# The denominator of linear attention, batches 3 to 7: from TensorE matmuls to GpSimd products and VectorE sums

## The chip, the cores and the metric

The kernel runs on one core of one Trainium2 chip. Its engines work side by side and meet at semaphores: PE (TensorE, matrix products into PSUM), DVE (VectorE), ACT (ScalarE), POOL (GpSimd) and SP (SyncE, which here only issues DMAs). The metric is the device time of one execution in microseconds; lower is better. The kernel before takes 287.69 us, the median of three runs (287.32 to 287.95).

## The reference

Linear attention over 8 batches, 8 heads, 576 tokens and 64 dimensions per head, and behind it a feed-forward layer over all 4608 tokens:

```python
def phi(x):
    return np.where(x > 0, x, np.exp(x) - 1.0) + 1.0
q_p, k_p = phi(q), phi(k)
kv  = np.einsum('bhsd,bhse->bhde', k_p, v)
z   = np.sum(k_p, axis=2)
num = np.einsum('bhsd,bhde->bhse', q_p, kv)
den = np.einsum('bhsd,bhd->bhs', q_p, z)[..., None] + 1e-06
x   = (num / den) reshaped to [4608 tokens, 512]
h   = x @ w_in              # 512 -> 2048
out = (h - np.tanh(h)) @ w_out   # 2048 -> 512
```

The denominator is one number for each token and head. It may divide `num` at the end, or, since `num` is linear in phi(q), it may divide phi(q) ahead of the product with kv.

## The kernel before

**The feed-forward part** goes over nine chunks (`c`) of 512 tokens. In the first half of a chunk, 16 slots (`s1[0]` to `s1[15]`, one for each 128 rows of h) hold four matmuls each (`l1mm`, line 366). After every second slot `l1act2` (lines 372 and 373) lets ACT take the tanh of a pair of PSUM banks and DVE subtract it into `gT`. The pairs go round in banks 0 to 5 of PSUM, so the matmuls of a pair need the subtraction of three pairs earlier. In the second half, 16 slots (`s2[0]` to `s2[15]`) hold four matmuls each (`l2mm`, line 387); after every fourth, `evac` copies a result out of PSUM on ACT (line 396) and SP sends it to DRAM (line 403).

**The attention part** of later batches is sewn into those slots. The lists `s1` and `s2` hold functions that issue their instructions behind the matmuls of a slot; each engine and each DMA queue works in that written order, so the order of the slots is the order of the work. With `n1 = c + 1` and `n2 = c + 2`, chunk c does this:

- At `s1[0]` GpSimd loads k, q and v of batch n2 (lines 87 and 90, a DMA with a cast to bf16). Ahead of the loads stands `gate` (line 383): GpSimd copies one element of the transposed q of batch n1, so the loads wait until that transpose has landed.
- At `s1[8]` (`s1[10]` in chunk 1) `a_den` makes the denominators of batch n1: 16 matmuls of a 128x32 stationary tile (line 287), then an addition of 1e-6 and a reciprocal on DVE (lines 292 and 296). `a_spread` sends the reciprocals to DRAM (`ds`, line 316) and reads them back, spread over the partitions, as `rdb` (line 319), by DMAs that SP issues.
- At `s2[2]` to `s2[8]` ACT and DVE make phi(k) and phi(q) of batch n2 (lines 129 to 131) and DVE copies v (`a_vp`, line 190). At `s2[8]` SP issues the DMA that transposes phi(q) of n2 into `qT` (`a_qT_dma`, line 148).
- At `s2[9]` (`s2[12]` in chunk 1) `a_num` has PE compute num of n1 from `qT` (lines 228 and 236), then kv and z of n2 (`kv_cols_mm`, line 177). DVE multiplies num by `rdb` on its way from PSUM to `xT` (lines 333 and 338), which drains PSUM banks 0 to 3 that the next chunk's first slots write. Last, `kz_copy` brings kv and z of n2 to SBUF; z is laid out as 32 columns by a product with a mask (line 199), kv is copied (line 200).

The next chunk's `l1mm` reads `xT` of batch n1. The buffers `kraw` and `qraw` are single, so a load of k or q can't begin before phi of the batch ahead has read them. Batches 0, 1 and 2 have paths of their own around chunks 0 and 1, which the change leaves as they are.

Of the kernel before, what the change touches and what calls it, by code (L numbers as in the profile page):

```python
# [11 lines left out]
F32 = mybir.dt.float32  # L12
# [6 lines left out]
def kernel(  # L19
# [9 lines left out]
    nc = tc.nc  # L29
# [5 lines left out]
    NF = DF // 128  # L35
    NC = N // 512
    J = S // 64


    const = ctx.enter_context(tc.tile_pool(name="const", bufs=1))  # L40
# [52 lines left out]
    def load_k(b):  # L93
        k_t[b] = kpool.tile([128, 2, 2, J, D], BF16, name="kraw")
        load(b, k_t[b], k, b == 0)

    def load_q(b):
        q_t[b] = kpool.tile([128, 2, 2, J, D], BF16, name="qraw")
        load(b, q_t[b], q, b == 0)

    def load_v(b):
        load(b, v_b[b % 2][:, 0:2], v, b == 0)
# [9 lines left out]


    kp_t, qp_t, qT_t, kz_t, rdb_t, rden_t = {}, {}, {}, {}, {}, {}

    def phi_pieces(b, src, store, name, i, parts=0):

# [22 lines left out]
    def a_qphi(b, i):  # L140
        phi(b, q_t, qp_t, "qp", i)
# [4 lines left out]
    def a_qT_dma(b):  # L146
        new_qT(b)
        nc.sync.dma_start_transpose(
            out=qT_t[b].rearrange("p i j g t -> p (i j) (g t)"),
            in_=qp_t[b].rearrange("p i j h d -> p (i j h d)"))  # L150
# [41 lines left out]
    def kv_cols_mm(b, b0, o):  # L192
        kz_t[b] = kz_c[b % 2]
        kv_mm(b, lambda rs, h, i, j: vp[rs, i, j, h, :],
              lambda cs, hg, i: ps_all[cs, b0 + hg, o + 66 * i:o + 66 * i + 66])

    def kz_copy(b, b0, o):
        ps = ps_all[:, b0:b0 + 2, o:o + 132].rearrange("p g (i e) -> p g i e", i=2)
        nc.vector.tensor_mul(kz_t[b][:, :, :, 64:96], ps[:, :, :, 64:65].to_broadcast([128, 2, 2, 32]), mask)
        nc.vector.tensor_copy(kz_t[b][:, :, :, 0:64], ps[:, :, :, 0:64])  # L200


    def b0_z(i):
# [74 lines left out]
    def a_den(b, bank, parts=range(4)):  # L278

        kz, qT = kz_t[b], qT_t[b]  # L280
        ps = ps_all[:, bank, 0:J * 16]
        for t in range(4) if b == 0 else ():
            nc.tensor.matmul(ps[32 * t:32 * t + 32], eps[:, 0:32], one[:, 0:J * 16], start=True, stop=False)
        for n, p in enumerate((0, 2, 1, 3)):
            if n in parts:
                for t in range(4):
                    nc.tensor.matmul(ps[32 * t:32 * t + 32], kz[:, p // 2, p % 2, 64:96],  # L287
                                     qT[:, p % 2, :, p // 2, 16 * t:16 * t + 16],
                                     start=(n == 0 and b > 0), stop=(n == NP - 1))
        if b > 0:  # L290
            den = rpool.tile([128, J * 16], F32, name="den")
            nc.vector.tensor_scalar(den, ps, 1e-6, None, ALU.add)
        else:
            den = ps
        rden = rpool.tile([128, J * 16], F32, name="rden")
        nc.vector.reciprocal(rden, den)  # L296
        rden_t[b] = rden
# [14 lines left out]
    def a_spread(b):  # L312

        ds = dram.tile([H, 4, J * 16], F32, name="ds")
        for t in range(4):
            nc.sync.dma_start(out=ds[:, t, :], in_=rden_t[b][32 * t:32 * t + H, :])
        rdb = rpool.tile([128, NP, 4, J, 16], F32, name="rdb")
        for hh in range(2):
            nc.sync.dma_start(
                out=rdb[64 * hh:64 * hh + 64].rearrange("p a t j c -> p (a t j c)"),  # L320
                in_=ds[4 * hh:4 * hh + 4].rearrange("h t c -> (h t c)").partition_broadcast(64))
        rdb_t[b] = rdb

    def a_num(b, nxt):

        rdb = rdb_t[b]
        for i in range(2):
            num_mm(b, i, lambda h: 2 * h + i)
        rest = rest_mm(b, 6, 0)
        if nxt:  # L330
            kv_cols_mm(nxt, 6, 128)
        for n in range(NP):
            nc.vector.tensor_mul(  # L333
                xT[:, n, S * b:S * b + 512].rearrange("p (j t c) -> p j t c", j=8, t=4),
                ps_all[:, n, :].rearrange("p (j t c) -> p j t c", j=8, t=4),
                rdb[:, n, :, 0:8, :].rearrange("p t j c -> p j t c"))
        for h in range(2):
            nc.vector.tensor_mul(
                xT[:, 2 * h:2 * h + 2, S * b + 512:S * b + 576].rearrange("p a (t c) -> p a t c", t=4),
                rest[h].rearrange("p a (t c) -> p a t c", t=4), rdb[:, 2 * h:2 * h + 2, :, 8, :])  # L340
        if nxt:
            kz_copy(nxt, 6, 128)

    def new_ns(b):

# [34 lines left out]
    def gate(qT):  # L380

        g0 = rpool.tile([1, 1], BF16, name="g0")
        nc.gpsimd.tensor_copy(g0, qT[0:1, 1, J - 1, 1, 63:64])  # L383
# [6 lines left out]
    def evac(c, i, o, f0=0, f1=None):  # L390
        f1 = DM if f1 is None else f1
        osb = opool.tile([128, DM], F32, name="osb")
        if f0:
            nc.vector.tensor_copy(osb[:, f0:f1], o[:, f0:f1])  # L394
        else:
            nc.scalar.copy(osb[:, f0:f1], o[:, f0:f1])  # L396

        last = c == NC - 1 and i == 3
        for half in range(2):
            b, j = divmod(2 * (4 * c + i) + half, J)  # L400
            cuts = [f0, 256, f1] if c == 3 and i < 3 else [f0, f1]
            for a0, a1 in zip(cuts, cuts[1:]):
                (nc.scalar if last and half else nc.sync).dma_start(
                    out=out[b * S:(b + 1) * S, a0:a1].rearrange("(p j) m -> p j m", j=J)[:, j, :],
                    in_=osb[64 * half:64 * half + 64, a0:a1])
# [103 lines left out]
    for c in range(NC):  # L509
# [4 lines left out]
        if c == 0:  # L514
            sub = {}

            def spread1(h):
                sub["bp"] = a_spread_pe(1, 4, (2 * h, 2 * h + 1))
                for p in (2 * h, 2 * h + 1):
                    a_scale(1, p, sub["ns"], sub["bp"], 144 * (p % 2))  # L520

            def num1():
                ns = sub["ns"] = new_ns(1)
                for h, ps in enumerate(rest_mm(1, 6, 128)):
                    nc.scalar.copy(ns[:, 2 * h:2 * h + 2, 8, :], ps)
                for i in range(2):
                    b0 = 4 + 2 * i
                    num_mm(1, i, lambda h: b0 + h)
                    nc.scalar.copy(ns[:, i::2, 0:8, :].rearrange("p a j t -> p a (j t)"), ps_all[:, b0:b0 + 2, :])

            s1[11].append(lambda: a_kphi(1, 0))
            s1[13].append(lambda: a_kphi(1, 1))
            s2[3].append(lambda: a_qphi(1, 0))
            s2[4].append(lambda: (a_qphi(1, 1), load_q(2), load_k(2), load_v(2)))
            s2[0].append(prepare)
            s2[7].append(lambda: (a_qT_pe(1, 0, Banks([4, 5])), a_kv(1, 6), a_qT_pe(1, 1, Banks([4, 5]))))
            s2[8].append(lambda: (scale_rest(0, 6, rdb_t[0]), a_den(1, 4), num1(), a_split(1)))
            s2[10].append(lambda: spread1(0))

            qs, ks = [], []  # L540

            def exp2(pieces, src, store, name, i):
                pieces.append(phi_pieces(2, src, store, name, i))
                pieces[i][0]()

            def rest2(f):
                f[1]()
                f[2]()

            s2[11].append(lambda: exp2(qs, q_t, qp_t, "qp", 0))  # L550
            s2[12].append(lambda: (spread1(1), exp2(qs, q_t, qp_t, "qp", 1), rest2(qs[0])))
            s2[13].append(lambda: (exp2(ks, k_t, kp_t, "kp", 0), rest2(qs[1]), a_qT_dma(2)))
            s2[14].append(lambda: rest2(ks[0]))
        elif n1 < B:
            if c == 1:
                s1[8].append(lambda: (kv_cols_mm(2, 6, 0), kz_copy(2, 6, 0)))
            s1[10 if c == 1 else 8].append(lambda: (a_den(n1, 6), a_spread(n1)))
            s2[12 if c == 1 else 9].append(lambda: a_num(n1, n2 if n2 < B else 0))
        if c == 1:
            s1[1].append(lambda: a_kphi(2, 1))  # L560
            s1[3].append(lambda: (a_vp(2, 0), a_vp(2, 1)))
        if c >= 1 and n2 < B:

            s1[0].append(lambda: (gate(qT_t[n1]), load_k(n2), load_q(n2), load_v(n2)))
            d = 2
            s2[d].append(lambda: a_kphi(n2, 0))
            s2[d + 2].append(lambda: a_kphi(n2, 1))
            s2[d + 4].append(lambda: a_qphi(n2, 0))
            s2[d + 6].append(lambda: (a_qphi(n2, 1), a_qT_dma(n2)))
            for i in range(2):  # L570
                s2[d + 1 + 2 * i].append(lambda i=i: a_vp(n2, i))
        if c == 0:
# [93 lines left out]
```

## Time and profile before

| | |
|---|---|
| median of the runs | 287.69 us (287.32 to 287.95) |
| the profiled execution's own time | 287.78 us |
| its span, first to last instruction | 286.0 us |
| mean granted TensorE clock | 0.998 |
| PE busy | 276.8 us (97%) |
| DVE busy | 171.3 us (60%) |
| ACT busy | 139.6 us (49%) |
| POOL busy | 30.0 us (10%) |
| GpSimd's DMA queue (loads), share of 16 DMA engines | 39.5% |
| SP's DMA queue (the rest), share of 16 DMA engines | 30.8% |

The profile is one execution of the program, with times in microseconds from the span's start. A group line gives the line of the code, the engine and operation, written and read tile, shape and count, then busy time and the mean duration in ns of one instruction, and behind the second bar the idle time just ahead of them and who ended it. The chain of waits is followed backwards from the last instruction. A timeline line gives start, duration, and in square brackets an idle time with what ended it. In a timeline's line for several instructions the duration is that from the start of the first to the end of the last. Neighbouring instructions of one engine can overlap by a little.

### The profile page before, as it was taken

What the parts mean: (1) busy time and instruction counts of PE and PEld (TensorE: products, weight loads), DVE (VectorE), ACT (ScalarE), POOL (GpSimd) and SP (SyncE); (2) the same over time, 40 slices, a digit from 0 to 9 for tenths busy, and PEclk for the clock granted to TensorE, in tenths of its full rate; (3) what the DMA queues carried; (4) which work ended last, traced back from release to release, by engine and by line L of the source; (5) the groups of instructions that cost most, each with busy time, mean ns of one, the idle gap of its engine ahead of it and who ended that gap; (6) DMA issues with size and microseconds to landing.
All of it is one profiled execution on the core that took longest, in us unless ns stands there. A gap on an engine that the chain in (4) does not pass through costs nothing.

```text
span 286.0 us, 5195 instructions
## 1 busy us (share of the span) xinstructions
PE 276.8 (97%) x2127; PEld 130.8 (46%) x2155; DVE 171.3 (60%) x271; ACT 139.6 (49%) x167; POOL 30.0 (10%) x50
## 2 busy tenths in 40 slices
PE   8889999999999999999999999999999999999995
PEld 3544464444444444445444544444444444444443
DVE  3749977997558782877277727874680467006600
ACT  4848557857335643564355625661551155126411
POOL 8642030120030003000300030000000000000000
PEclk9999999999999999999999999999999999999999
DMA  6999999997979668955996679656126210230032
GB/s 98 197 206 213 208 207 208 233 179 147 235 148 207 162 102 151 222 127 132 147 208 148 145 142 216 148 126 138 39 75 138 68 37 0 52 82 16 0 76 73
DMA packets 39496, 38.99 MB, mean 136 GB/s; under 512 B 16368, under 2 KB 34608, under 8 KB 38704
## 3 DMA queue, kind: packets, MB, share of 16 engines
q0 software_dynamic: 17488, 18.35, 39.5%
q1 hardware_dynamic: 21824, 20.17, 30.8%
q8 instruction: 17, 0.28, 0.4%
q10 hardware_dynamic: 160, 0.13, 0.1%
q14 instruction: 7, 0.06, 0.1%
HBM read 43.91 MB, written 9.55 MB: 187 GB/s over the span
## 4 chain that ended last, share of the span: by engine, by line
PE 93%; DMA 2%; issue 1%; POOL 1%; DVE 1%; DVEq 0%; POOLq 0%
PE ps_all L366 43%; PE ps_all L387 42%; DMA v<-in_v_dram 2%; PE ps_all L177 2%; PE ps_all L228 1%; PE ps_all L622 1%; PE ps_all L287 1%; PE ps_all L251 1%; POOL kraw L87 1%; DVE xT L255 0%; POOL qraw L87 0%; PE ps_all L159 0%; DVE rden L296 0%; PE ps_all L236 0%; PE ps_all L354 0%
## 5 line engine op out<-in xcount | busy, mean ns | idle before, releaser
L366 PE MATMUL ps_all<-xT,w_in_sb 128*128 128x512 bf16 x559 | 125.4, 379 | 1.2 <-issue 0.5
L387 PE MATMUL ps_all<-w_out_sb,gT 128*128 128x512 bf16 x547 | 122.2, 379 | 1.3 <-issue 1.0
L373 DVE TENSOR_TENSOR gT<-ps_all,th 128x1024 bf16<-128x1024 f32 x64 | 77.8, 1217 | 66.7 <-ACT th L372 66.7
L372 ACT ACTIVATE th<-ps_all 128x1024 f32<-128x1024 f32 x64 | 65.5, 1023 | 50.1 <-PE ps_all L366 50.1
L366 PEld LDWEIGHTS <-w_in_sb 128*128 128x128 bf16 x574 | 55.4, 98 | 67.1 <-issue 0.6
L387 PEld LDWEIGHTS <-gT 128*128 128x128 bf16 x560 | 54.1, 98 | 64.4 <-issue 0.2
L396 ACT COPY osb<-ps_all 128x512 f32<-128x512 f32 (+1 forms) x36 | 20.8, 582 | 74.0 <-PE ps_all L387 49.0
L129 ACT ACTIVATE e<-qraw 128x1152 bf16<-128x1152 bf16 x16 | 18.5, 1160 | 8.4 <-DMA qraw<-in_q_dram 8.4
L333 DVE TENSOR_TENSOR xT<-ps_all,rdb 128x512 bf16<-128x512 f32 x24 | 14.9, 681 | 9.1 <-PE ps_all L228 6.7
L129 ACT ACTIVATE e<-kraw 128x1152 bf16<-128x1152 bf16 x15 | 17.4, 1161 | 0.4 <-DMA kraw<-in_k_dram 0.4
L131 DVE TENSOR_TENSOR qp<-e,r 128x1152 bf16<-128x1152 bf16 x16 | 12.1, 758 | 6.0 <-ACT e L129 5.1
L131 DVE TENSOR_TENSOR kp<-e,r 128x1152 bf16<-128x1152 bf16 x15 | 11.4, 758 | 5.9 <-ACT e L129 4.9
L383 POOL COPY g<-qT 1x1 bf16<-1x1 bf16 x5 | 0.9, 177 | 115.1 <-DMA qT<-qp 115.1
L378 DVE TENSOR_TENSOR gT<-ps_all,th 128x512 bf16<-128x512 f32 x16 | 10.3, 685 | 2.6 <-ACT th L377 2.0
L377 ACT ACTIVATE th<-ps_all 128x512 f32<-128x512 f32 x16 | 9.2, 598 | 4.9 <-PE ps_all L366 3.7
L449 PE MATMUL ps_all<-zero 128*128 128x512 bf16 x29 | 8.7, 460 | 1.2 <-DVE zero L408 1.2
L130 DVE TENSOR_SCALAR r<-qraw 128x1152 bf16<-128x1152 bf16 x16 | 7.5, 468 | 3.0 <-DMA qraw<-in_q_dram 3.0
L296 DVE RECIPROCAL rden<-den 128x144 f32<-128x144 f32 x7 | 7.4, 1053 | 0.2
L394 DVE COPY osb<-ps_all 128x128 f32<-128x128 f32 x1 | 0.3, 290 | 11.6 <-PE ps_all L622 11.6
L130 DVE TENSOR_SCALAR r<-kraw 128x1152 bf16<-128x1152 bf16 x15 | 6.8, 450 | 0.0
L90 POOL DMA_DIRECT2D qraw<-in_q_dram x7 | 5.2, 749 | 13.7 <-DVE r L130 13.0
L177 PEld LDWEIGHTS <-kp 64*64 64x64 bf16 x504 | 5.5, 105 | 0.6 <-DVE vp L190 0.4
(83 smaller groups left out, 111.9 us busy)
## 6 DMA issues: line engine op xcount, KB each, us to landing
out_dram<-osb SPq DMA_DIRECT2D x64, 128.0 KB
rdb<-ds SPq DMA_DIRECT2D x12, 576.0 KB
kraw<-in_k_dram POOLq DMA_DIRECT2D x7, 576.0 KB, 6.6
qraw<-in_q_dram POOLq DMA_DIRECT2D x7, 576.0 KB, 8.6
v<-in_v_dram POOLq DMA_DIRECT2D x7, 576.0 KB, 11.1
w_in_sb<-in_moe_w_in_dram POOLq DMA_DIRECT2D x3, 512.0 KB, 13.4
w_out_sb<-in_moe_w_out_dram POOLq DMA_DIRECT2D x3, 512.0 KB, 19.4
out_dram<-osb SPq DMA_DIRECT2D x12, 64.0 KB
```

The costliest lines, as they stand in the source:

```text
L129: return (lambda: nc.scalar.activation(e, x, AF.Exp), lambda: nc.vector.tensor_scalar(r, x, 0.0, 1.0, ALU.max, ALU.add), lambda: nc.vector ...
L130: lambda: nc.vector.tensor_scalar(r, x, 0.0, 1.0, ALU.max, ALU.add),
L131: lambda: nc.vector.tensor_tensor(y, e, r, ALU.min))
L177: nc.tensor.matmul(ps_of(cs, hg, i), kp[rs, i, j, h, :], v_of(rs, h, i, j), start=(j == 0), stop=(j == J - 1))
L333: nc.vector.tensor_mul(xT[:, n, S * b:S * b + 512].rearrange("p (j t c) -> p j t c", j=8, t=4), ps_all[:, n, :].rearrange("p (j t c) -> p ...
L366: nc.tensor.matmul(h, w_in_sb[:, p, fi * 128:(fi + 1) * 128], xT[:, p, c * 512:(c + 1) * 512], start=(n == 0), stop=(n == NP - 1))
L372: nc.scalar.activation(th, h, AF.Tanh)
L373: nc.vector.tensor_sub(gT[:, fi:fi + 2, :], h, th)
L377: nc.scalar.activation(th, h, AF.Tanh)
L378: nc.vector.tensor_sub(gT[:, fi, :], h, th)
L387: nc.tensor.matmul(o, gT[:, fi, i * 128:(i + 1) * 128], w_out_sb[:, fi, :], start=(fi == 0), stop=(fi == NF - 1))
L396: nc.scalar.copy(osb[:, f0:f1], o[:, f0:f1])
```

## The change

For batches 3 to 7 (`b >= QS`, with `QS = 3`) the denominator is made without PE:

- `kz_copy` copies z of the batch (128x4 numbers) to SBUF on DVE, SP writes it to DRAM (`zs`), and two further DMAs of SP read it back, repeated over 64 partitions each (`zb`).
- `q_prod`, at `s1[1]` of chunk n1 - 1, multiplies phi(q) by `zb` on GpSimd, in two instructions of 128x1152 elements, into an f32 tile `pr`.
- `q_den`, four times, at `s1[3]`, `s1[5]`, `s1[7]` and `s1[9]`, sums `pr` over d on DVE (128x9 sums of 64).
- `q_scale`, at `s1[9]`, adds 1e-6, takes the reciprocal of 128x36 numbers on DVE, multiplies phi(q) by it in place on GpSimd (two instructions of 128x1152 elements), and then issues the transposing DMA, which before stood at `s2[8]` of the chunk ahead.
- `a_num` copies num from PSUM to `xT`, half on DVE and half on ACT, with no product.
- The gate ahead of the loads is there in chunk 1 alone. `a_den` and `a_spread` are left out for these batches.
- Of the output DMAs of chunk 3 one fewer is cut in two.

```diff
     def kz_copy(b, b0, o):
...
+        if b < QS:
+            nc.vector.tensor_mul(kz_t[b][:, :, :, 64:96], ..., mask)
+        else:
+            z = rpool.tile([128, 2, 2], F32, name="z")
+            nc.vector.tensor_copy(z, ps[:, :, :, 64])
+            zs = dram.tile([2, 2, 128], F32, name="zs")
+            nc.sync.dma_start(out=zs.rearrange("g i x -> x g i"), in_=z)
+            zb_t[b] = rpool.tile([128, 2, 128], F32, name="zb")
+            for g in range(2):
+                nc.sync.dma_start(out=zb_t[b][64 * g:64 * g + 64].rearrange("p i x -> p (i x)"),
+                                  in_=zs[g].rearrange("i x -> (i x)").partition_broadcast(64))
         nc.vector.tensor_copy(kz_t[b][:, :, :, 0:64], ps[:, :, :, 0:64])
+    def q_prod(b):
+        pr_t[b] = rpool.tile([128, 2, J, 2, D], F32, name="pr", tag="rdb")
+        dn_t[b] = rpool.tile([128, 2, J, 2], F32, name="dn")
+        for i in range(2):
+            nc.gpsimd.tensor_mul(pr_t[b][:, i].rearrange("p j h d -> p j (h d)"),
+                                 qp_t[b][:, i].rearrange("p j h d -> p j (h d)"),
+                                 zb_t[b][:, i].unsqueeze(1).to_broadcast([128, J, 128]))
+    def q_den(b, i, h):
+        nc.vector.tensor_reduce(dn_t[b][:, i, :, h], pr_t[b][:, i, :, h, :], mybir.AxisListType.X, ALU.add)
+    def q_scale(b):
+        dn = dn_t[b].rearrange("p i j h -> p (i j h)")
+        nc.vector.tensor_scalar(dn, dn, 1e-6, None, ALU.add)
+        rd = rpool.tile([128, 2, J * 2], F32, name="rd")
+        nc.vector.reciprocal(rd.rearrange("p i x -> p (i x)"), dn)
+        for i in range(2):
+            x = qp_t[b][:, i].rearrange("p j h d -> p (j h) d")
+            nc.gpsimd.tensor_mul(x, x, rd[:, i].unsqueeze(2).to_broadcast([128, J * 2, D]))
+        a_qT_dma(b)
     def a_num(b, nxt):
...
+        if b >= QS:
+            for h, copy in enumerate((nc.vector.tensor_copy, nc.scalar.copy)):
+                copy(xT[:, 2 * h:2 * h + 2, S * b:S * b + 512], ps_all[:, 2 * h:2 * h + 2, :])
+                copy(xT[:, 2 * h:2 * h + 2, S * b + 512:S * b + 576], rest[h])
+        else:
+            num_scale(b, rest)
...
-            cuts = [f0, 256, f1] if c == 3 and i < 3 else [f0, f1]
+            cuts = [f0, 256, f1] if c == 3 and 2 * i + half < 5 else [f0, f1]
...
-            s1[10 if c == 1 else 8].append(lambda: (a_den(n1, 6), a_spread(n1)))
+            if n1 < QS:
+                s1[10].append(lambda: (a_den(n1, 6), a_spread(n1)))
+            else:
+                for n in range(4):
+                    s1[3 + 2 * n].append(lambda n=n: q_den(n1, n // 2, n % 2))
+                s1[9].append(lambda: q_scale(n1))
...
+        if QS <= n1 < B:
+            s1[1].append(lambda: q_prod(n1))
...
-            s1[0].append(lambda: (gate(qT_t[n1]), load_k(n2), load_q(n2), load_v(n2)))
+            if c == 1:
+                s1[0].append(lambda: gate(qT_t[n1]))
+            s1[0].append(lambda: (load_k(n2), load_q(n2), load_v(n2)))
...
-            s2[d + 6].append(lambda: (a_qphi(n2, 1), a_qT_dma(n2)))
+            s2[d + 6].append(lambda: a_qphi(n2, 1))
```

More of the change, by code (lines that the diff above doesn't have):

```diff
@@ L37 @@
     J = S // 64
+    QS = 3
     const = ctx.enter_context(tc.tile_pool(name="const", bufs=1))
@@ L114 @@
     kp_t, qp_t, qT_t, kz_t, rdb_t, rden_t = {}, {}, {}, {}, {}, {}
+    zb_t, pr_t, dn_t = {}, {}, {}
     def phi_pieces(b, src, store, name, i, parts=0):
@@ L198, in kz_copy @@
         ps = ps_all[:, b0:b0 + 2, o:o + 132].rearrange("p g (i e) -> p g i e", i=2)
-        nc.vector.tensor_mul(kz_t[b][:, :, :, 64:96], ps[:, :, :, 64:65].to_broadcast([128, 2, 2, 32]), mask)
-        nc.vector.tensor_copy(kz_t[b][:, :, :, 0:64], ps[:, :, :, 0:64])
+        if b < QS:
+            nc.vector.tensor_mul(kz_t[b][:, :, :, 64:96], ps[:, :, :, 64:65].to_broadcast([128, 2, 2, 32]), mask)
+        else:
[7 more added lines that the diff above has]
+                                  in_=zs[g].rearrange("i x -> (i x)").partition_broadcast(64))
+        nc.vector.tensor_copy(kz_t[b][:, :, :, 0:64], ps[:, :, :, 0:64])
+    def q_prod(b):
[16 more added lines that the diff above has]
+        a_qT_dma(b)
     def b0_z(i):
@@ L324, in a_num @@
     def a_num(b, nxt):
-        rdb = rdb_t[b]
         for i in range(2):
@@ L331, in a_num, with num_scale @@
             kv_cols_mm(nxt, 6, 128)
+        if b >= QS:
[4 more added lines that the diff above has]
+            num_scale(b, rest)
+        if nxt:
+            kz_copy(nxt, 6, 128)
+    def num_scale(b, rest):
+        rdb = rdb_t[b]
         for n in range(NP):
@@ L340, in a_num @@
                 rest[h].rearrange("p a (t c) -> p a t c", t=4), rdb[:, 2 * h:2 * h + 2, :, 8, :])
-        if nxt:
-            kz_copy(nxt, 6, 128)
     def new_ns(b):
```

## The prediction

> **What bounds the kernel now.** I read the page first: engines, the slices, the chain.
>
> ```profile
> PE 276.8 (97%) x2127; PEld 130.8 (46%) x2155; DVE 171.3 (60%) x271; ACT 139.6 (49%) x167; POOL 30.0 (10%) x50
> ...
> DMA  6999999997979668955996679656126210230032
> ...
> PE 93%; DMA 2%; issue 1%; POOL 1%; DVE 1%; DVEq 0%; POOLq 0%
> ```
>
> PE is the bound nearly everywhere, so only PE work taken away, or a new PE wait, moves the time. The DMA row has slices of 7.15 us; the eleventh (71.5 to 78.7 us) stands at 9 tenths or more. Next, the chain of waits around one denominator:
>
> ```profile
> 115.68 2.11 PE ps_all L366 x9
> 117.79 0.36 PE ps_all L287 x16
> 118.15 5.29 PE ps_all L366 x24
> ```
>
> The 16 matmuls of `a_den` are on the chain with 0.36 us. In the timeline they are 0.43 us busy, start to end. Now chunk 3 in the timeline, where batch 4 is finished; it gives the deadlines.
>
> ```profile
> 109.85 7.93 PE L366 MATMUL ps_all<-xT,w_in_sb 128*128 128x512 bf16 x35
> ...
> 114.56 1.22 DVE L373 TENSOR_TENSOR gT<-ps_all,th 128x1024 bf16<-128x1024 f32 x1 [0.50 <-ACT th L372]
> ...
> 119.49 1.05 DVE L296 RECIPROCAL rden<-den 128x144 f32<-128x144 f32 x1
> ...
> 124.14 8.80 PE L387 MATMUL ps_all<-w_out_sb,gT 128*128 128x512 bf16 x40
> ...
> 132.86 0.63 PE L228 MATMUL ps_all<-qT,kz 64*64 64x512 bf16 x8
> ...
> 134.72 3.00 SPq L148 DMA_TRANSPOSE qT<-qp  x1
> ...
> 139.91 0.18 POOL L383 COPY g<-qT 1x1 bf16<-1x1 bf16 x1 [27.61 <-DMA qT<-qp]
> ```
>
> Counted from the chunk's first matmul (109.85), the second half begins at 14.29 and num at 23.01. Without the 0.43 us of the denominator these become 13.86 and 22.6: by 22.6 the transposed q must lie in SBUF. The last two lines price the transpose: 5.2 us from issue to the gate (other batches: 4.1 to 6.9). Last, the handover from chunk 1 to chunk 2, the first that the change touches:
>
> ```profile
> 63.31 1.65 SPq L316 DMA_DIRECT2D ds<-rden  x4
> 68.82 1.12 SPq L319 DMA_DIRECT2D rdb<-ds  x2
> ...
> 77.08 2.48 DVE L333 TENSOR_TENSOR xT<-ps_all,rdb 128x512 bf16<-128x512 f32 x4 [2.38 <-DMA rdb<-ds]
> 79.48 0.48 DVE L338 TENSOR_TENSOR xT<-ps_all,rdb 128x128 bf16<-128x128 f32 x2
> ...
> 80.36 1.89 PE L366 MATMUL ps_all<-xT,w_in_sb 128*128 128x512 bf16 x8
> ...
> 81.63 0.18 POOL L383 COPY g<-qT 1x1 bf16<-1x1 bf16 x1 [22.83 <-DMA qT<-qp]
> ```
>
> DVE waits for `rdb` of batch 2 until 77.08 and has written `xT` at 79.96, only 0.4 us ahead of chunk 2's first matmul. The loads of batch 4 stand behind the gate, at 81.63, and so stay clear of `rdb`.
>
> **Removed.** Five denominators of 0.36 to 0.43 us on PE; I take 0.40, so 2.0 us. The reciprocal (1.05) and addition (0.30) of 144 columns leave DVE. Five `rdb` round trips leave the queue of SP. None of these but the PE time is on the chain.
>
> **Num copied plainly: nothing on the path.** Four products of 0.68 us and two of 0.28 become, on DVE, about 1.2 us for 1024 columns (L373's 1.22 reads as many from PSUM) and 0.28; ACT does as much (its 128x1024 copies from PSUM take 1.01) in the gap of 3.2 us that it has there. PSUM is drained 1.5 us sooner. Were ACT's gap gone, `evac` would be 1.3 us later, behind which only an output buffer waits.
>
> **DVE's sums.** A sum over 128x576 f32 lies nearest to L359 (128x576, 0.75 us); the bounds are 0.3 (twice the rate) and 1.1. With the 0.08 us by which neighbours overlap it costs 0.67, and a subtraction 1.14, so 1.81 a pair against PE's 1.73: four pairs run up 0.3 us of lag. By the timeline's pairs the reciprocal (36 columns, a quarter of 1.05 and a fixed part: 0.35) then ends at 12.4, and the subtraction that frees bank 4 for the second half at 13.6 against 13.86. It just fits. What is queued behind a late `q_den` are those subtractions, and for them waits PE: the first sum may start no later than 6.2 without a stall.
>
> **GpSimd's products.** No row shows one. POOL's memset of 128x1152 (one write) took 1.08 us, the lower bound; three times that for two reads and a write, 3.25, is the upper. I take the middle, 2.2, since nothing is nearer. The Trainium skill's GPSIMD Engine Reference speaks against the placement: "Elementwise — side-by-side cycle accounting" measures 4497 ns for 2048 elements with two inputs, about twice VectorE, and section 4.1 says to use VectorE. An estimate from it is 2.5 us for 1152 elements, 0.6 us more for two. No run here shows it yet.
>
> **The way from reciprocal to transpose.** `q_scale` waits on DVE, then two products: 12.4 + 0.1 + 4.4 = 16.9. SP's transpose now waits for GpSimd, and the output DMAs of the second half's first `evac` are queued behind it (harmless, five output buffers). With 0.1 and 5.2 for the transpose q lies ready at 22.2 against 22.6: hidden, with 0.4 us to spare. By the page's 2.5 us it would be 22.8, that is 0.2 us late in each chunk.
>
> **The way of z.** In place of the masked product (0.28) DVE copies 128x4 numbers, about 0.15, nearest to the 128x8 rows. After num's copies z is ready 4.2 us ahead of the chunk (104.11 + 1.4 + 0.15 is 105.66, the chunk 109.85). Then: issue 0.3 (L316 issues four in 1.3 to 1.65); waiting until `zs` lies in DRAM; two broadcasts to issue, 1.1 (L319's 1.12); their landing; one product, 2.2. The wait has rows, from the end of L316 to the start of L319: 1.1 to 2.1 us where no loads run, 3.9 in the fence above (64.96 to 68.82), when loads were in flight, and 4.4 at the start. Without the gate, loads start once phi has read `kraw` and `qraw`, some 9 and 6 us ahead of the chunk; the three loads took 11 us and more, so they lie across z's way in chunks 3 to 5. I take 3.9 for the wait, and 2.0 for the landing (same bounds, 1.1 to 4.4; 131 KB is far less than `rdb`). The first product ends at -4.2 + 0.3 + 3.9 + 1.1 + 2.0 + 2.2 = 5.3 against 6.2: hidden. Both at their worst would be 8.4 with a product of 2.2, a stall of 2.2 us. The writes of `zs` are 512 single numbers; the skill's "DMA: Bandwidth & Descriptors", "Rules for kernel authors", says that a non-contiguous last dimension makes one descriptor per element and should be avoided. No row here has such a transfer, so the sum goes by `ds`.
>
> **Chunk 2 pays.** There batch 2 still needs `rdb`, and num stands at `s2[12]`, so z comes late. Two steps:
>
> - Loads of batch 4, freed of the gate, start at about 70.7 (k) and 74 (q), when `kraw` and `qraw` have been read, in the slice that is already full. `rdb` (68.82 to 77.08) shares the engines with them. A load of k alone takes 6.6 us; the delay lies between 0 (the transpose of batch 3 at 74.77 leaves) and 6.6. I take 2.5, less the 0.4 of slack: PE's chunk 2 starts 2.1 later, at 82.5.
> - z is ready at 80.1 + 2.5 = 82.6. With 0.3 + 3.9 + 1.1 + 2.0 + 2.2 the first product ends at 92.1. The deadline is 82.5 + 6.2 = 88.7: a stall of 3.4 us, from 0 (unloaded rows, no delay of `rdb`: 80.1 + 0.3 + 1.1 + 1.1 + 1.1 + 2.2 = 85.9 against 86.6) to 6.
>
> **Sum.** 287.78 (the profiled execution, 1.78 over its span of 286.0) - 2.0 + 2.1 + 3.4 = 291.3. The median of the runs lies 0.09 below that execution: 291.2.
>
> **Rivals.** *A, all hidden, faster.* Loads don't hurt `rdb` and z, because SP's small transfers find room; then the five denominators are pure gain: 285.7, and up to 287.1 if chunk 2 stalls for a little. For it: chunks 3 to 6 fit by my sums, and ten broadcasts of 576 KB (`rdb`) are gone. Against: the full slice at 71.5.
>
> *B, late in every chunk, slower.* GpSimd's products take 3.0 or more, or GpSimd and DVE's phi work hinder each other (the trace has them nowhere side by side), or the next load of k meets the transpose. With 3.0, q lies ready at 12.4 + 0.1 + 6.0 + 0.1 + 5.2 = 23.8, 1.2 late; with the slowest transpose (6.9) 2.9 late. In chunks 3 to 6 that is 4.8 to 11.6 on top of 291.2: 296 to 303. It decides from a product of 2.4 us upward.
>
> *C, the two cancel.* Chunk 2 loses just what five denominators bring: 287.7.
>
> **Chances.** Forecast 0.41 (its own range 288.4 to 294), A 0.33, B 0.2, C 0.06. So faster 0.33, same 0.06 (0.2% is 0.6 us, about what a measurement of this kernel can tell from no change), slower 0.61. For eight in ten the range takes A whole and the nearer part of B: 285.6 to 298.
>
> **What would show it.** Right: no L287 beyond batch 2 in chunks 2 to 6; PE idle at chunk 2's start, released by DVE's L333, and again near its eleventh slot, behind a DVE wait for POOL; chunks 3 to 6 at about 29.1 us with no PE wait at L228. Wrong towards A: `rdb` lands by 77 all the same and the first sum of chunk 2 starts by 86.6. Wrong towards B: products over 2.4 us and PE waiting for `qT` ahead of L228 in each chunk.

## The result and the profile after

The changed kernel takes 334.77 us, the median of its runs (333.31 to 336.0), against 287.69: 1.164 times as long, with a 95% interval of 1.159 to 1.169. The profiled execution took 333.31 us, its span is 331.5. The forecast was 291.2, its range ended at 298. The sign was right; the size was not: 47.1 us lost where 3.5 were forecast.

The page of the changed kernel, engines and chain of waits (the lines that answer to those of before):

```profile
PE 285.1 (86%) x2047; PEld 132.5 (40%) x2075; DVE 173.0 (52%) x271; ACT 145.6 (44%) x177; POOL 74.1 (22%) x66
...
PEclk9999999999956999689996999769997999999999
...
PE 48%; DMA 33%; DVE 6%; POOL 6%; ACT 3%; issue 1%; SPq 1%; POOLq 0%
PE ps_all L410 23%; PE ps_all L431 23%; DMA zs<-z 18%; DMA v<-in_v_dram 7%; DMA zb<-zs 5%; POOL pr L220 4%; DMA w_in_sb<-in_moe_w_in_dram 3%; DMA out_dram<-osb 2%; DVE gT L417 2%; ACT e L131 1%; ACT osb L440 1%; DVE dn L225 1%; DVE xT L368 1%; DVE qp L133 1%; DVE xT L379 1%
```

PE has fallen from 97% to 86% of a longer span. The chain, 93% on PE before, runs over DMAs for a third, and one transfer alone, `zs<-z`, holds 18% of the span: 2 KB, written five times. The clock row has dips that before had not. (In this file `l1mm` is line 410, the subtraction 417, `l2mm` 431, num 263 and 271, `kz_copy`'s three DMAs 207 and 210, the products 220, the sums 225, the scaling 234, the transpose 150.)

Who waited for whom (total in us, times, longest):

```profile
POOL pr L220 <- DMA zb<-zs: 92.9, 5, 22.2
...
DVE dn L225 <- POOL pr L220: 42.5, 5, 13.2
...
PE ps_all L410 <- DVE gT L417: 37.9, 5, 12.3
```

Read from top to bottom: z arrives late, GpSimd's product is late, DVE stands at the first sum, and the subtractions queued behind it keep PE from its banks. Five waits, one for each batch. Chunk 3 in the timeline, to be laid beside the fence of before:

```profile
119.02 0.15 DVE L205 COPY z<-ps_all 128x4 f32<-128x4 f32 x1
...
119.20 0.39 SPq L207 DMA_DIRECT2D zs<-z  x1
...
123.43 8.80 PE L410 MATMUL ps_all<-xT,w_in_sb 128*128 128x512 bf16 x39
...
130.79 1.11 SPq L210 DMA_DIRECT2D zb<-zs  x2
...
134.93 4.71 POOL L220 TENSOR_TENSOR pr<-qp,zb 128x1152 f32<-128x1152 bf16 x2 [16.18 <-DMA zb<-zs]
137.33 0.76 DVE L225 TENSOR_REDUCE dn<-pr 128x9 f32<-128x576 f32 x1 [7.96 <-POOL pr L220]
138.00 1.22 DVE L417 TENSOR_TENSOR gT<-ps_all,th 128x1024 bf16<-128x1024 f32 x1
...
139.27 6.99 PE L410 MATMUL ps_all<-xT,w_in_sb 128*128 128x512 bf16 x24 [7.04 <-DVE gT L417]
...
144.23 4.20 POOL L234 TENSOR_TENSOR qp<-qp,rd 128x1152 bf16<-128x1152 bf16 x2 [4.59 <-DVE rd L231]
...
148.45 1.81 SPq L150 DMA_TRANSPOSE qT<-qp  x1
...
154.82 0.63 PE L263 MATMUL ps_all<-qT,kz 64*64 64x512 bf16 x8
```

SP could issue the broadcasts only at 130.79, that is 11.6 us after it had issued `zs`. The first product ends 13.9 us after the chunk's first matmul; the prediction's deadline was 6.2, so a stall of 7.7 is due, and PE waited 7.04. In batches 3 to 7 `zs` took 13.5, 11.6, 11.8, 12.4 and 9.0 us from its issue to the next, and PE's waits were 12.3, 7.0, 7.2, 7.6 and 3.8.

The waits are not all. PE's clock by stretches, behind two of the waits (columns: stretch and its length, busy time and count of PE, PEld, DVE, ACT, POOL, then the granted clock, DMA share and GB/s):

```profile
101.10:104.70 3.60, 3.60 (x9) 1.27 (x9) 3.60 (x5) 1.03 (x2) 0.36 (x1) 0.50 0.00 0
104.70:108.20 3.50, 3.50 (x16) 1.52 (x15) 2.66 (x5) 2.04 (x2) 2.12 (x2) 0.94 0.03 5
...
139.30:142.80 3.50, 3.50 (x9) 1.21 (x9) 3.50 (x5) 1.02 (x1) 0.34 (x1) 0.52 0.00 0
142.80:146.00 3.20, 3.20 (x17) 1.47 (x15) 2.67 (x5) 2.05 (x2) 1.77 (x1) 1.00 0.00 0
```

After each wait PE runs some 3.5 us at half its clock. The 24 matmuls left of the first half then take 7.30, 6.99, 6.70, 8.11 and 7.03 us instead of 5.2 (24 by 0.216, the step from one matmul to the next at full clock): 10.2 us in all.

### The profile page after: what moved, and what is told of

It reads as the page before. It is cut to its first block, busy times and chain, and to the rows that moved or that the text cites. A ratio compares the mean times of both kernels' runs of the same rounds, so it can differ in the third digit from the quotient of the medians.

```text
span 331.5 us, 5039 instructions
## 1 busy us (share of the span) xinstructions
PE 285.1 (86%) x2047; PEld 132.5 (40%) x2075; DVE 173.0 (52%) x271; ACT 145.6 (44%) x177; POOL 74.1 (22%) x66
## 4 chain that ended last, share of the span: by engine, by line
PE 48%; DMA 33%; DVE 6%; POOL 6%; ACT 3%; issue 1%; SPq 1%; POOLq 0%
PE ps_all L410 23%; PE ps_all L431 23%; DMA zs<-z 18%; DMA v<-in_v_dram 7%; DMA zb<-zs 5%; POOL pr L220 4%; DMA w_in_sb<-in_moe_w_in_dram 3%; DMA out_dram<-osb 2%; DVE gT L417 2%; ACT e L131 1%; ACT osb L440 1%; DVE dn L225 1%; DVE xT L368 1%; DVE qp L133 1%; DVE xT L379 1%
## 5 line engine op out<-in xcount | busy, mean ns | idle before, releaser
L410 PE MATMUL ps_all<-xT,w_in_sb 128*128 128x512 bf16 x562 | 135.0, 399 | 38.7 <-DVE gT L417 37.9
L410 PEld LDWEIGHTS <-w_in_sb 128*128 128x128 bf16 x574 | 58.1, 102 | 113.2 <-issue 51.9
L220 POOL TENSOR_TENSOR pr<-qp,zb 128x1152 f32<-128x1152 bf16 x10 | 23.6, 2371 | 92.9 <-DMA zb<-zs 92.9
L225 DVE TENSOR_REDUCE dn<-pr 128x9 f32<-128x576 f32 x20 | 14.9, 747 | 42.5 <-POOL pr L220 42.5
L234 POOL TENSOR_TENSOR qp<-qp,rd 128x1152 bf16<-128x1152 bf16 x10 | 21.0, 2118 | 23.0 <-DVE rd L231 13.8
L91 POOL DMA_DIRECT2D kraw<-in_k_dram x7 | 5.4, 773 | 24.7 <-ACT e L131 18.8
L368 DVE CAST xT<-ps_all 128x1024 bf16<-128x1024 f32 x5 | 6.1, 1219 | 6.9 <-PE ps_all L271 6.9
L368 ACT CAST xT<-ps_all 128x1024 bf16<-128x1024 f32 x5 | 5.1, 1012 | 4.4 <-PE ps_all L271 3.8
```

What stands on the lines that cost most here:

```text
L91: nc.gpsimd.dma_start(out=t.rearrange("q h i j d -> q (h i) (j d)"), in_=x.rearrange("(n q) x -> q n x", n=4))
L220: nc.gpsimd.tensor_mul(pr_t[b][:, i].rearrange("p j h d -> p j (h d)"), qp_t[b][:, i].rearrange("p j h d -> p j (h d)"), zb_t[b][:, i].uns ...
L225: nc.vector.tensor_reduce(dn_t[b][:, i, :, h], pr_t[b][:, i, :, h, :], mybir.AxisListType.X, ALU.add)
L234: nc.gpsimd.tensor_mul(x, x, rd[:, i].unsqueeze(2).to_broadcast([128, J * 2, D]))
L368: copy(xT[:, 2 * h:2 * h + 2, S * b:S * b + 512], ps_all[:, 2 * h:2 * h + 2, :])
L410: nc.tensor.matmul(h, w_in_sb[:, p, fi * 128:(fi + 1) * 128], xT[:, p, c * 512:(c + 1) * 512], start=(n == 0), stop=(n == NP - 1))
```

## The experiments

**Is it the number of pieces, the loads, or a fixed time?** z lies in SBUF as four numbers a partition and goes to DRAM in the order g, i, x, so that neighbours in SBUF are 512 bytes apart there: 512 pieces of 4 bytes. The first theory was that their number is dear. Rivals: the loads that lost their gate, or a fixed time of every small write.

```diff
# 128 runs of 16 bytes
-zs = dram.tile([2, 2, 128], F32); dma(out=zs.rearrange("g i x -> x g i"), in_=z)
+zs = dram.tile([128, 4], F32);    dma(out=zs, in_=z as [x, (g i)])
```

> zs is written as 128 runs of 16 bytes (each partition its four numbers side by side) and read back in that order, so the products use z in a wrong order; all instructions and waits stay. Theory (the write is slow because it consists of 512 single numbers): from issue to landing zs falls from 9.0 (batch 7, no loads in flight) to 2 to 3 us, and from 11.6 to 13.5 (batches 3 to 6) to 4 to 7; PE's five stalls on gT (37.9 us) fall to 5 to 18, total 293 to 310. Rival 1 (the loads that lost their gate hold the write up): the write stays over 9 us in batches 3 to 6, total over 325. Rival 2 (a fixed time of a small write to DRAM): all five stay at 9 or more, total about 334.

295.8 us (a single execution, and so are the four other runs on the shape of the write that follow). `zs` took 1.9 us for batch 7, 5.0 to 5.9 for batches 3 to 6; PE's waits on the subtraction fell from 37.9 to 7.4 us, 4.2 of them in chunk 2. Batch 7 in SP's timeline (line 207 writes `zs`, 210 waits for it):

```profile
202.53 0.34 SPq L207 DMA_DIRECT2D zs<-z  x1
204.40 1.11 SPq L210 DMA_DIRECT2D zb<-zs  x2
```

A fixed time is out: three quarters and more of the 47 us are in the shape of this one 2 KB write. What the loads add on top is seen in the difference between batch 7 and the others.

```diff
# loads behind the products
-s1[0].append(lambda: (load_k(n2), load_q(n2), load_v(n2)))
+s1[0 if c == 1 else 2].append(lambda: (load_k(n2), load_q(n2), load_v(n2)))
```

> The loads of batch n2 are issued at s1[2], behind the products of batch n1 on GpSimd, so no load is in flight while zs and zb move (chunks 2 to 5). Theory (512 single numbers): zs still takes about 9 us in every batch, as in batch 7; the stalls fall by the 2.5 to 4.5 us that the loads added, 10 to 16 us in all, but the loads now come late and phi(k) at s2[2] may wait; total 318 to 335. Rival 1 (loads): zs lands within 1 to 3 us in every batch, the stalls of chunks 3 to 6 vanish, total under 305.

325.1 us. With no load in flight `zs` still took 8.5 to 10.4 us in every batch. So the loads are worth some 8 to 10 of the 47 us (325.1 against 333.31 of the profiled execution and 334.77 of the median), and the rest stays without them.

**Number or size?** Two runs vary one of them each: 128 single numbers (one of the four is written), and 512 runs of 16 bytes (each number four times).

> Only one of the four numbers of each partition is written: zs is 128 single numbers of 4 bytes (three quarters of z are left out; zb repeats what was written). Beside the run with 128 runs of 16 bytes (landing 1.9 us for batch 7, 5.0 to 5.9 for batches 3 to 6 with loads in flight). Theory (the number of pieces decides): the same landings, 1.5 to 2.5 and 4.5 to 6.5, total 293 to 298. Rival (a piece of 4 bytes is dear by its size): batch 7 takes well over 1.9 us, 3 or more, and the others 6 or more.

> z is copied four times side by side, and zs is written as 512 runs of 16 bytes in the scattered order of the change (the broadcasts read the first 512 numbers, so the products use wrong values). Theory (the number of pieces decides): landing about 9 us for batch 7 and 11 to 14 for the others as in the changed kernel, total 325 to 340. Rival (a piece of 4 bytes is dear by its size): landings near those of 128 runs of 16 bytes, 2 to 6 us, total under 305.

Batch 7, where no load is in flight, in SP's timeline: the changed kernel,

```profile
234.42 0.39 SPq L207 DMA_DIRECT2D zs<-z  x1
243.44 1.11 SPq L210 DMA_DIRECT2D zb<-zs  x2
```

128 single numbers,

```profile
241.60 0.34 SPq L207 DMA_DIRECT2D zs<-z  x1
249.85 1.31 SPq L210 DMA_DIRECT2D zb<-zs  x2
```

and 512 runs of 16 bytes:

```profile
213.98 0.39 SPq L207 DMA_DIRECT2D zs<-z  x1
217.22 1.11 SPq L210 DMA_DIRECT2D zb<-zs  x2
```

9.0, 8.3 and 3.2 us. A quarter of the pieces saved almost nothing, and four times the bytes in as many pieces landed almost three times as fast (307.1 us for the whole). The run with 128 numbers took 342.9 us, more than the changed kernel itself: its broadcasts read `zs` in another form and landed in 4.1 to 5.2 us from their issue, against 2.5 to 3.7 in the changed kernel. My theory fell: it isn't the number. Two explanations were left: a piece of 4 bytes is slow as such, or such pieces hinder each other because many lie side by side in one stretch of DRAM (16 in each 64 bytes, against 4 with runs of 16 bytes). The last run of this row puts the 512 numbers 64 bytes apart:

```diff
-zs = dram.tile([2, 2, 128], F32);  dma(out=zs.rearrange("g i x -> x g i"), in_=z)
+zs = zs_c[b % 2]      # [512, 16] f32, zeroed at the start
+dma(out=zs.rearrange("(g i x) w -> x g i w", g=2, i=2)[:, :, :, 0:1], in_=z.unsqueeze(3))
```

> The 512 single numbers of z are written 64 bytes apart in DRAM (two buffers of 32 KB, zeroed at the start) instead of side by side; the broadcasts read the first 512 numbers of the buffer, so the products use mostly zeros. So far: 4-byte pieces side by side land in 8.3 to 9.0 us for batch 7 whether there are 128 or 512 of them, 16-byte pieces in 1.9 (128) and 3.2 us (512). Theory (4-byte pieces that lie side by side hinder each other, many to one stretch of DRAM): 512 pieces now land like those of 16 bytes, 3 to 4 us for batch 7 and 7 to 9 for the others; total 300 to 312. Rival (a piece of 4 bytes is dear by its size alone): 8 us and more for batch 7, 10 to 13 for the others; total 325 or more.

```profile
214.25 0.38 SPq L212 DMA_DIRECT2D zs<-z  x1
216.37 1.11 SPq L215 DMA_DIRECT2D zb<-zs  x2
```

2.1 us for batch 7, and 307.8 us in all. As many pieces, as small, issued in the same 0.38 us: their neighbourhood in DRAM changed, and seven of nine microseconds are gone. (The buffers were also zeroed at the start, which no run varied by itself; the 128 runs of 16 bytes landed in 1.9 us without it.) That settles what the rows can settle: 4-byte writes side by side hinder each other. What in the memory or the DMA engines does it was not tried. The Trainium skill's "DMA: Bandwidth & Descriptors", under "Specifications", says that below 512 B a transfer is read, modified and written; that would fit, but the page doesn't say that neighbours matter, and no run shows the mechanism. With loads in flight this form too takes 7.4 to 8.8 us (512 runs of 16 bytes: 7.4 to 8.9, 128 runs: 5.0 to 5.9), so with loads in flight the number of pieces does seem to count.

**The rest of the sum, without z.** The products take a constant tile; the copy of z and its DMAs are gone.

> Leaves out z altogether: the products use a constant tile, and the copy of z and its three DMAs are gone. Theory (only the way of z costs): the gain of the five denominators shows unhindered, 285.5 to 286.5, no PE wait on gT or qT over 0.5 us in chunks 2 to 6. Rival (GpSimd and the transpose late): PE waits at the num matmuls of chunks 2 to 6, 290 or more. If the loads without a gate hurt rdb of batch 2 as the prediction has it, chunk 2 starts 2 us late: about 288.

285.86 us, 0.993 of before (0.992 to 0.995). PE in the timeline (first half of chunks 3, 5 and 6):

```profile
109.24 13.98 PE L404 MATMUL ps_all<-xT,w_in_sb 128*128 128x512 bf16 x63
...
167.35 13.98 PE L404 MATMUL ps_all<-xT,w_in_sb 128*128 128x512 bf16 x63
...
196.35 13.98 PE L404 MATMUL ps_all<-xT,w_in_sb 128*128 128x512 bf16 x63
```

A chunk is 29.0 us long instead of 29.5, and in chunks 2 to 6 the profile has no wait of PE for `gT` or `qT`. GpSimd's products, DVE's sums, the scaling, the late transpose and the loads without a gate all fit. So the whole loss sits in the way of z. The rival "late in every chunk through GpSimd" is out, and so is a late `rdb`.

**The gate alone.** The kernel before, with the one edit that the gate stays in chunk 1 only.

> The kernel before with one edit of the change alone: the gate ahead of the loads stays in chunk 1 only. The prediction's step: the loads of batch 4 meet rdb of batch 2, which lands 2.5 us later, chunk 2 starts 2.1 us late, 289 to 291. Rival (rdb is not held up, since in the changed kernel DVE waited for PE there and not for rdb): same as before within 0.6 us; a gain is not expected.

290.82 us, 1.010 of before (1.007 to 1.013): the forecast number, but by another way. SP and PE in that run:

```profile
74.39 11.34 SPq L148 DMA_TRANSPOSE qT<-qp  x1
...
90.39 0.43 PE L287 MATMUL ps_all<-qT,kz 128*32 128x144 bf16 x16 [2.48 <-DMA qT<-qp]
```

`rdb` was in time. The transpose of batch 3 met the loads: SP was 11.3 us in issuing it (3.3 before), and PE's denominator waited 2.5 us for `qT`. In the kernel before, the gate guards the transpose. In the changed kernel the transpose comes later than the loads that cross the chunk's start, so that they don't hold it up: the profile after shows 3.9 to 5.1 us from its issue to its landing. What the loads cost there falls on `zs`, as the run with the loads behind the products showed.

**Mending z.** Four versions keep the change and send z another way. First over PE: DVE multiplies the identity by z, PE spreads the result against ones, ACT copies it to SBUF.

```diff
+nc.vector.tensor_mul(dg, ident broadcast over (g, i), z broadcast over columns)   # 128x512 bf16
+for i, g: nc.tensor.matmul(ps_all[64*g:64*g+64, 6+i, 264:392], one[:, 0:64], dg[:, g, i, :])
+nc.scalar.copy(zb, ps_all[:, 6:8, 264:392])
```

> z goes no way over DRAM: DVE multiplies the identity by z (128x512, bf16), PE spreads it with four matmuls of 128 columns against ones, ACT copies the result to SBUF as zb; all else stays as in the changed kernel. Theory (only the way of z over DRAM costs; the other steps of the prediction fit their deadlines): no PE wait on gT over 1 us in chunks 2 to 6, 0.2 to 0.4 us of PE work a chunk in place of 0.40, total 286 to 289. Rival (GpSimd's two products and the transpose are late in every chunk as well): PE waits at the num matmuls in chunks 3 to 6, 1 us or more each, total 292 or more.

288.13 us, 1.002 of before (1.001 to 1.003). No wait of PE for `gT` or `qT` in chunks 2 to 6, as the theory has it, and the last matmuls of the profile begin at 277.84 instead of 278.92; but the four matmuls take back 0.3 of the 0.47 us of a chunk, and the end of the output DMAs came 0.9 us later relative to PE (SP's last wait was 2.1 us, 1.2 before). Why the end differs stays open.

> z spread by PE as before, but with two matmuls of 256 columns (one for each half of the partitions) in place of four of 128. If the two halves of the array work side by side as they did, 0.1 us less PE time in each of chunks 2 to 6, half a us in all: 287.3 to 287.9 against 287.6 to 287.8 of the kernel before. Rival (PE isn't what holds that version, the end of the output DMAs is): 288.0 or more, as with four matmuls.

289.1 us, 1.004 (1.001 to 1.007), runs from 287.59 to 293.56. Its chunks are as long as with four matmuls (29.3 us), so nothing was saved; in one chunk PE waited 0.95 us for `qT`. Where the spread of its runs comes from stays open.

Then over DRAM, in runs of 16 bytes, one broadcast of all 512 numbers, GpSimd picking each half's, loads behind the products, and batch 3's kv and z three slots earlier:

> The way of z mended without PE: zs is written as 128 runs of 16 bytes, one broadcast brings all 512 numbers to every partition, GpSimd picks each half's 256 (two copies), loads are issued behind the products (k, v, q), and in chunk 1 kv and z of batch 3 are made at s2[9] instead of s2[12]. Theory (only the way of z costs; 128 runs with no loads in flight land in 1.9 us): zb lands by 2 us after the chunk's first matmul, no stall on gT over 0.5 us in chunks 3 to 6, total 285.7 to 287.5. Rival (loads behind the products now come late, or meet the transpose): PE waits at the num or kv matmuls of chunks 2 to 5, 0.5 us or more each, total 288 to 292.

287.85 us, 1.001 (0.999 to 1.003): no difference. `zs` took 1.5 to 2.5 us in chunks 2 to 5 (4.6 in chunk 1), and no wait of PE on the subtraction is left in its list of waits (the first half of chunk 2 is 0.25 us longer than with a constant z), but the rival had a point: loads and transpose now meet, and PE waits for `qT` in chunk 3.

```profile
133.01 0.63 PE L266 MATMUL ps_all<-qT,kz 64*64 64x512 bf16 x8 [0.68 <-DMA qT<-qp]
```

So the loads of k and v were put between the two products, that of q behind the second:

> As the version with 128 runs of 16 bytes and one broadcast, but the loads of k and v are issued between the two products and that of q behind the second, about 2 us sooner, so that less of them is in flight when SP issues the transpose. Theory (the transpose is held up by loads in flight, 0.7 us of PE wait in chunk 3): no PE wait on qT, 286.0 to 287.0, faster than the kernel before. Rival (the second product, 1.5 us later, holds up the third sum): PE waits on gT of 0.3 to 1 us in chunks 2 to 5, 287.5 to 289.

287.16 us, 0.998 of before (0.996 to 1.000, just below one): the best that kept the whole computation, by half a microsecond. In its profile PE waits on `qT` no longer; 0.25 and 0.48 us of waits on the subtraction are left, in chunk 2.

## Why the prediction was wrong, step by step

- **The step that failed** is "No row here has such a transfer, so the sum goes by `ds`". From the issue of `zs` to the issue of the broadcasts the sum had 0.3 + 3.9 = 4.2 us, and 0.3 + 4.4 = 4.7 at the worst; measured were 9.0 to 13.5. The rows of `ds` are runs of 576 bytes (64 at the start). I had the sentence on single numbers before me, and let it change neither the value nor the upper end: a bound taken from rows that lack the very property that is new was no bound. The reason that the prediction cites, one descriptor for each element, would not have given the size either: with a quarter of the elements it took 8.3 us instead of 9.0. What the runs showed in its place: 4-byte pieces side by side in DRAM are slow, and the same pieces 64 bytes apart take 2.1 us.
- **A term that the sum lacked.** The sum priced a wait of PE at its length alone. Each of the five was followed by some 3.5 us at about half clock, about 2 us more. By the measured terms: 5 x 0.47 = 2.35 gained, 37.9 of waits, 10.2 of slow restarts: 287.78 - 2.35 + 37.9 + 10.2 = 333.5, against 333.31 measured.
- **Chunk 2, first step (`rdb` late by 2.5): wrong.** Chunk 2 began at 80.00, 0.4 us sooner than before. In the fence below, of the changed kernel, DVE waits for PE there, not for `rdb`; `rdb` landed 7.7 us after its issue, in spite of the full slice. The busy share of the engines did not say which transfer would suffer: without the gate it was the transpose, not `rdb`.

```profile
76.80 2.48 DVE L379 TENSOR_TENSOR xT<-ps_all,rdb 128x512 bf16<-128x512 f32 x4 [2.46 <-PE ps_all L271]
```

- **Chunk 2, second step (z late there): right in place, far too small**, 3.4 forecast and 12.3 measured.
- **The deadlines were right.** 6.2 for the first product foretold each wait within about a microsecond once the arrival of z was known; num's 22.6 was met with a constant z and with the four matmuls, with no wait for `qT` in the list of waits.
- **GpSimd's products:** 2.2 taken, 2.37 (products) and 2.12 (scaling) measured; the 2.5 that the prediction estimated from the Trainium skill's GPSIMD Engine Reference was somewhat high. DVE's sums took 0.75, the row L359 to the digit. The transpose took 3.9 to 5.1 (with a constant z up to 5.6), 5.2 taken. The landing of the broadcasts took 2.2 to 3.1, 2.0 taken. The gain of the denominators was 0.47 a chunk, 0.40 taken.
- **Two slips that changed no term.** Both waits at their worst give -4.2 + 0.3 + 4.4 + 1.1 + 4.4 + 2.2 = 8.2, not 8.4, so a stall of 2.0. And of the rows read as "where no loads run", those of 1.8 and 1.9 us stand where the chunk's loads were just ending (DMA share 0.48 and 0.37).
- **Rival A** (all hidden, 285.7) is what the kernel does when z costs nothing: 285.86. **Rival B** named the right pattern, a stall in each chunk, but from the wrong engine, and at a tenth to a quarter of the price.

## What to carry to other kernels

Where a change brings a transfer whose piece size or layout no row of the profile has, its worst case is not the worst of other rows: ask first what the new layout does, and measure that transfer by itself. Small results that go over DRAM should be written in the order in which they lie in SBUF, in runs, and sorted behind the landing; if single numbers must be written, space them. And a stall of a busy PE of two microseconds and more can cost more than its length, so a wait that "just fits" deserves its margin.

## What the runs showed of the hardware

- 4-byte writes side by side in DRAM: 128 of them took 8.3 us and 512 took 9.0; the same 512 spaced by 64 bytes 2.1, 128 runs of 16 bytes 1.9, 512 such runs 3.2 (no loads in flight). With loads in flight these times rise by 2.1 to 6.6 us.
- A DMA transpose beside which three loads start (the kernel before without its gate): SP's issue alone took 7.4 to 11.3 us, against 1.9 to 3.3. Where the loads had been issued 7 to 9 us earlier (loads behind the products, runs of 16 bytes) it took 2.7 to 3.5.
- The clock: in the changed kernel, after PE waits of 3.8 us and more, it stood at 0.50 to 0.60 for some 3.5 us; after 0.3 us (128 runs of 16 bytes) it stood at 1.00. Between them the length alone does not decide: with 512 runs of 16 bytes it stood at 0.53 over 3.5 us after a wait of 2.6 and at 0.64 over 3.4 us after one of 2.2, while with single numbers 64 bytes apart it stayed at 1.00 after two waits of 2.4. The Trainium skill's "TensorE: Matmul & The Clock Gate", Part 1, has the array fall to half rate after an idle window of about 3.4 us and recover after as long a busy one. The recovery agrees; the fall came after shorter waits too, here in the run without the gate, 0.65 over 3.6 us after a wait of only 2.5 us:

```profile
87.90:90.40 2.50, 0.02 (x4) 0.04 (x4) 1.22 (x1) 0.21 (x1) 0.00 (x0) 1.00 1.21 281
90.40:94.00 3.60, 3.60 (x26) 1.53 (x26) 2.32 (x3) 1.02 (x1) 0.00 (x0) 0.65 0.19 65
```
